# Weight pieces stored one place later in the queue, and weight sums computed in the second pass too

## The chip, the cores and the metric

The kernel runs on one core of one Trainium2 chip. The metric is device time in microseconds (us) of one execution, the median of the runs shown. A core has five engines that work side by side, each through its own instructions in order: TensorE (PE in the profile; PEld is its weight load), VectorE (DVE), ScalarE (ACT), GpSimd (POOL) and SyncE (SP), which here does little but issue transfers. Engines wait for each other, and for transfers, by semaphores. An instruction that waits holds up everything behind it on its engine.

## The reference

Three stages follow one another, all in float32:

```python
scores = scale * (q @ k.T) * Dmat          # retention: decay gamma_h ** (i - j), causal
x = (scores @ v) -> 2304 rows of 512
p = domain_probs / domain_probs.sum(-1)
x1 = sum over 4 experts e of p[:, e] * (relu(x @ w1[e]) @ w2[e])      # 512 -> 1024 -> 512
logits = x1 @ w_gate                        # second layer: 8 experts, 288 rows each,
out[rows of e] = relu(x1[rows] @ w1[e]) @ w2[e]    # assigned by descending logits
```

## The kernel before

To keep float32 accuracy on TensorE, every operand of a large product is split into a high half and the remainder, its low half; a product is then three products. A split is a ScalarE copy (the high half) and a subtraction on GpSimd or VectorE (the low half).

The work has three stages: the retention (up to some 107 us of the span), the first expert layer (to about 860 us), and the routed second layer. The change touches the first expert layer only. It runs in three passes, u = 0, 1 and 2, over 768 rows each. A pass has 16 *pairs*, k = 16u to 16u + 15; a pair is one block of 256 hidden columns of one expert. All 16 blocks of w1 are the same in each pass, so block q % 16 is fetched again in each.

The first product x @ w1 is done with seven block products instead of eight, over sums of blocks of x and sums of blocks of w1. The steps of a pair are called a to g (`step`, L697); each is one product of six matmuls, accumulating into PSUM tiles P, Q and R. Between them stand `keep` (L683, ScalarE copies P into `sum1` to `sum3`: keep 1 after a, keep 2 after c, keep 3 after e) and `add` (VectorE adds a kept sum to Q or R). P must be kept before the next product is accumulated into it, so step c waits for keep 1, step e for keep 2 and step f for keep 3. `y_next` (L837) puts a tile of the second product (12 matmuls, L727) between b and c, between d and e and between e and f.

**Weights of the first product.** `w1_load(q)` (L372) is issued at the end of pair q - 2. In the first pass it fetches the two raw blocks r1 from `w1a`. `w1_ops(q)` (L386) then makes six tiles: `wah`/`wal` from the first block, `wbh`/`wbl` from a sum held in place in the second block, `wth`/`wtl` from three sums in `tw` (128 x 768). Its first steps are `wah` and four VectorE subtractions (L397), which make the sums. `w1_store(q)` (L381) writes the sums to the scratch tensor `ts`. In the second and third passes `w1_load` fetches the first raw block, and the sums from `ts` (one 128 x 512 and one 128 x 768 transfer), and `w1_ops` returns six steps instead of ten: `steps[:1] + steps[5:]`. The calls `some(3)`, `some(3)`, `some(2)`, `some(2)` emit the steps after c, after d, after e and before f. The r1 tiles have two buffers for two blocks, so the next `w1_load` waits until the low halves of the block before are made; `tw` has one.

**Pieces of the second layer's weights.** While the first two passes run, all weights of the second layer are split ahead of time: 128 pieces of 128 x 512, 64 in each pass, by the generator `halves` (L436). For piece c it copies the high half on ScalarE (`pair`, L447), makes the low half on GpSimd (L448), then issues the store of piece c - 1 (L453 or L455) and the load of piece c + 2 into `pv` (L433). Both tiles have three buffers. `spare(main)` (L854) is called nine times in a pair, before and after most steps; five of these calls have main true, and each advances `halves` by one piece. The calls with main false do something only in the third pass.

Other transfers on SyncE's queue in a pair: two raw w2 blocks (`w2_load`, L659, k and 0 after step b, k and 1 ahead of step c), the loads and stores of `block_sums` (L866, called by `more_sums` after steps c and f), and the rows of x1 at the end of a pass. The order of all this is written out by hand in the loop over k (L898). At the *turn*, the last pair of a pass (`turn_`), the pieces must be done, and the x blocks of the next pass are loaded and split.

Of the kernel before, what the change touches and what calls it, by code (L numbers as in the profile page):

```python
# [144 lines left out]
class Graph:  # L145
# [87 lines left out]
    def copy(self, out, x, func=AF.Copy, part=False):  # L233
        self.add("act", 0.08 + self.size(x) / 1200.0, lambda: self.nc.scalar.activation(out, x, func), (x,), (out,),
                 part=part)
# [92 lines left out]
def tile_kernel(ctx, tc, a, x1d, xs, ss, ts, w1s, w2s, out):  # L328
    nc = tc.nc
# [16 lines left out]
    if True:  # L346
# [23 lines left out]
        WO, R1, TW = {}, {}, {}  # L370

        def w1_load(q, which=(0, 1)):  # L372
            e, j = divmod(q % 16, 4)
            for i in which:
                R1.setdefault(q, {})[i] = wl.tile([128, 512], F32, name="r1", bufs=2)
                nc.sync.dma_start(R1[q][i], a["w1a"][e, 2 * j + i] if q < 16 or i == 0 else ts[q % 16, :, :512])
            if q >= 16:
                TW[q] = wl.tile([128, 768], F32, name="tw")
                nc.sync.dma_start(TW[q], ts[q % 16, :, 512:])

# [5 lines left out]
        def w1_ops(q):  # L386
            ra, rb = (lambda: R1[q][0]), (lambda: R1[q][1])
            b11, b21, b12, b22 = (lambda: ra()[:, :256]), (lambda: ra()[:, 256:]), (lambda: rb()[:, :256]), (lambda: rb()[:, 256:])

            def w(i, h):  # L390
                if q not in WO:
                    WO[q] = [[wl.tile([128, n], F32R, name=f"w{x}{y}", bufs=2) for y in "hl"]
                             for x, n in (("a", 512), ("b", 512), ("t", 768))]
                return WO[q][i][h]

            t = lambda i: tt()[:, i * 256:(i + 1) * 256]
            sub = lambda e, o, x, y: lambda: e.tensor_tensor(o(), x(), y(), op=OP.subtract)  # L397
            copy = lambda i, x: lambda: nc.scalar.activation(w(i, 0), x(), AF.Copy)  # L398
            low = lambda e, i, x: lambda: e.tensor_tensor(w(i, 1), x(), r32(w(i, 0)), op=OP.subtract)  # L399
            v, p = nc.vector, nc.gpsimd  # L400

            def tt():
                if q not in TW:
                    TW[q] = wl.tile([128, 768], F32, name="tw")
                return TW[q]

            steps = [("act", 0.51, copy(0, ra), ("ra",), (f"wah{q}",)),
                    ("v", 0.33, sub(v, lambda: t(0), b12, b11), ("ra", "rb"), ("tw0",)),
                    ("v", 0.33, sub(v, b12, b22, b12), ("rb",), ("rb",)),
                    ("v", 0.33, sub(v, lambda: t(1), b22, lambda: t(0)), ("rb", "tw0"), ("tw1",)),  # L410
                    ("v", 0.33, sub(v, lambda: t(2), b21, lambda: t(1)), ("ra", "tw1"), ("tw2",)),
                    ("pool", 1.18, low(p, 0, ra), ("ra", f"wah{q}"), (f"wal{q}",)),
                    ("act", 0.72, copy(2, tt), ("tw0", "tw1", "tw2"), (f"wth{q}",)),
                    ("v", 0.86, low(v, 2, tt), (f"wth{q}", "tw0", "tw1", "tw2"), (f"wtl{q}",)),
                    ("act", 0.51, copy(1, rb), ("rb",), (f"wbh{q}",)),
                    ("pool", 1.18, low(p, 1, rb), ("rb", f"wbh{q}"), (f"wbl{q}",))]
            return steps if q < 16 else steps[:1] + steps[5:]

        hp = pool(st_l, "hp")
        st_p = ExitStack()  # L420
# [5 lines left out]
        def piece_of(c):  # L426
            e, i = divmod(c // 2, 8)
            return e, i, slice(c % 2 * HW, c % 2 * HW + HW)

        def halves_load(c):  # L430
            e, i, o = piece_of(c)
            r = room[0].tile([128, HW], F32, name="pv")
            nc.sync.dma_start(r, (a["w1b"] if i < 4 else a["w2b"])[e, i % 4][:, o])  # L433
            HV[c] = r

        def halves(c0, c1, loaded=False):  # L436

            if not loaded:
                for c in range(c0, min(c0 + HA, c1)):
                    halves_load(c)  # L440
                yield
                yield
            for c in range(c0, c1 + 1):
                if c < c1:
                    r = HV[c]
                    pair = HV[c] = room[0].tile([128, 2, HW], F32R, name="pair")
                    nc.scalar.activation(pair[:, 0], r, AF.Copy)  # L447
                    nc.gpsimd.tensor_tensor(pair[:, 1], r, r32(pair[:, 0]), op=OP.subtract)  # L448
                if c > c0:
                    e, i, o = piece_of(c - 1)  # L450
                    pair = HV.pop(c - 1)
                    if i < 4:
                        nc.sync.dma_start(w1s[e, i][:, :, o], r32(pair))  # L453
                    else:
                        nc.sync.dma_start(w2s[e, i - 4][:, o], r32(pair[:, 1]))  # L455
                if c + HA < c1:
                    halves_load(c + HA)
                yield


        with ExitStack() as st:
# [152 lines left out]
            for i in (0, 1, 4, 3, 5, 2, 6):  # L614
                for op in x_split(xr, i, LOW[i]):
                    g.add(*op)
            g.floor = 50.0
            g.add("sp", 0.8, lambda: w1_load(0), (), ("ra", "rb"))
            for op in w1_ops(0):
                g.add(*op)  # L620
            g.bias = 0.0
            late_sp = [g.add("sp", 1.0, lambda: w1_store(0), ("rb", "tw0", "tw1", "tw2"), ())]
            late_sp.append(g.add("sp", 0.8, lambda: w1_load(1), (), ("ra", "rb")))
            for op in w1_ops(1):
                g.add(*op)
            late_sp.append(g.add("sp", 1.0, lambda: w1_store(1), ("rb", "tw0", "tw1", "tw2"), ()))
            late_sp.append(g.add("sp", 0.8, lambda: w1_load(2), (), ("ra", "rb")))
            for n in range(HA):
                late_sp.append(g.add("sp", 0.4, lambda n=n: halves_load(n), (), ()))
# [8 lines left out]
        with ExitStack() as st:  # L638
# [17 lines left out]
            def w2_load(q, i):  # L656
                e, j = divmod(q % 16, 4)
                W2[q, i] = [hp.tile([128, 512], F32, name="r2", bufs=2)]
                nc.sync.dma_start(W2[q, i][0], a["w2a"][e, 2 * j + i])  # L659
# [190 lines left out]
            later = late()  # L850
            HC = 64
            jobs = [halves(0, HC, True), halves(HC, NH)]

            def spare(main):  # L854

                if not open_ or k < 2:
                    return
                if k > 16 * NP1 - 16:
                    next(later, None)
                elif main:  # L860
                    next(jobs[min(u, 1)], None)


            BLOCKS = {0: (0, 0), 1: (0, 1), 2: (1, 1)}
# [33 lines left out]
            for k in range(NPAIR):  # L898
                u, kk = divmod(k, 16)
                turn_ = kk == 15 and u < NP1 - 1  # L900
                lone = k in (0, NPAIR - 2)
                early = w1_ops(k + 1) if 1 <= k < NPAIR - 1 else []

                def more_sums():
# [7 lines left out]
                def block(i):  # L912
                    raw[i] = room[0].tile([128, 2, TG], F32, name=f"raw{i}")
                    if i in BLOCKS:
                        row, col = BLOCKS[i]
                        nc.sync.dma_start(raw[i], xs[u, :, 2 * col:2 * col + 2, row * TG:(row + 1) * TG])
                    else:
                        nc.sync.dma_start(raw[i], ss[u, i - 3])
# [7 lines left out]
                if k not in (1, NPAIR - 1):  # L926
                    step(k, "a")
                if turn_:
                    for _ in jobs[u]:
                        assert False  # L930
                    for _ in sums_of[u]:
                        assert False
                    st_p.close()
                    open_ = False
                    room[0] = pool(st_p, f"blocks{u}")
                    w2_load(k, 0)
                    for i in (0, 1, 4):
                        block(i)
                full = lone
                if k:  # L940
                    put(k - 1, 0, 1, "R")
                spare(True)
                step(k, "b")
                if not turn_:
                    w2_load(k, 0)
                spare(False)
                put(k, 0, 0, "Q")
                if not open_ and kk == 0:
# [4 lines left out]
                if turn_:  # L953
                    for i in (3, 5, 2, 6):
                        block(i)
                spare(True)
                step(k, "c")
                some(10 if full else 3)
# [76 lines left out]
    with ExitStack() as st:  # L1035
# [388 lines left out]
        for n, t in enumerate(range(NT - LATE, NT)):  # L1424
# [10 lines left out]
            else:  # L1435
                x = last[t - NT + K1]
# [80 lines left out]
```

## Time and profile before

| | us |
|---|---|
| Timed runs | 1154.66, 1157.22, 1160.98 (median 1157.22) |
| Profiled execution, its own time | 1154.98 |
| Span from the first to the last instruction | 1153.2 |
| TensorE busy | 1133.4 (98%) |
| TensorE weight load busy | 988.5 (86%) |
| VectorE busy | 705.6 (61%) |
| GpSimd busy | 632.0 (55%) |
| ScalarE busy | 561.2 (49%) |

The shares are averages over stages with different limits. The matmuls' ends are modelled, so a busy TensorE is not a TensorE at its peak: a weight load that comes late can lengthen a product without showing as idle time. The chain of work that ended last leads through TensorE's products in the third pass, and through transfers (w2 blocks, `pv` pieces, `tw`) in the first two.

### The profile page before, as it was taken

The page shows a single profiled execution, that of the slowest core. Times are in us where ns is not written, and L with a number is a line of the kernel's source. Part 1 is how long each engine was busy: PE and PEld are TensorE (multiplying, and loading weights), DVE is VectorE, ACT ScalarE, POOL GpSimd, SP SyncE. Part 2 cuts the span into 40 slices and gives each one's busy share as a digit, 9 for nine tenths or more (in the row PEclk, how much of TensorE's full clock was granted, in tenths as well). Part 3 has the DMA queues.
Part 4 walks back from the last instruction along what each step waited for, and adds up shares of the span by engine and source line. Part 5 has one row for each costly group of instructions (what it writes and reads, how often), then busy time and mean ns, then how long its engine had stood idle before and what let it go on. Part 6 is the DMA issues. An engine that isn't in the chain of part 4 may idle for free.

```text
span 1153.2 us, 22293 instructions
## 1 busy us (share of the span) xinstructions
PE 1133.4 (98%) x8007; PEld 988.5 (86%) x8007; DVE 705.6 (61%) x1632; ACT 561.2 (49%) x1262; POOL 632.0 (55%) x563
## 2 busy tenths in 40 slices
PE   9999999999999999999999999999999999999997
PEld 7878899989898998988899999998987888788886
DVE  4696777767665444544456777776347766666421
ACT  3444555555565555555554666666430333333341
POOL 4551576677774576666645999998231112222311
PEclk9999999999999999999999999999999999999999
DMA  9675699999994889898974655555214877788690
GB/s 330 219 248 176 234 338 344 322 319 321 345 309 144 279 286 335 290 310 302 316 262 158 221 181 195 192 180 158 78 55 167 311 292 284 307 332 334 252 409 27
DMA packets 131056, 292.99 MB, mean 254 GB/s; under 512 B 14849, under 2 KB 26881, under 8 KB 126849
## 3 DMA queue, kind: packets, MB, share of 16 engines
q1 hardware_dynamic: 127584, 281.88, 69.3%
q0 software_dynamic: 3216, 9.67, 2.4%
q8 instruction: 63, 1.03, 0.4%
q14 instruction: 49, 0.39, 0.1%
q10 hardware_dynamic: 144, 0.02, 0.0%
HBM read 214.41 MB, written 77.33 MB: 253 GB/s over the span
## 4 chain that ended last, share of the span: by engine, by line
PE 56%; DMA 15%; issue 5%; POOL 5%; DVE 3%; ACT 3%; SPq 3%; POOLq 0%; ACTq 0%; DVEq 0%
PE py L727 16%; PE ph L227 10%; PE P L677 9%; PE py L227 8%; PE R L677 5%; DMA r<-in_w2a 4%; DMA pv<-in_w1b 3%; DMA pv<-in_w2b 3%; DMA tw<-w_sums 3%; PE Q L677 2%; POOL pair L448 2%; PE pr L227 2%; DMA r<-in_w1a 1%; POOL w2l L665 1%; ACT pair L447 1%
## 5 line engine op out<-in xcount | busy, mean ns | idle before, releaser
L727 PE MATMUL py<-w2h,h 128*128 128x512 f32 x1056 | 349.5, 391 | 0.9 <-ACT h L694 0.8
L727 PEld LDWEIGHTS py<-w2h,h 128*128 128x128 f32 x1056 | 198.2, 188 | 40.4 <-ACT h L694 1.7
L448 POOL TENSOR_TENSOR pair<-pv,pair 128x512 fp32r<-128x512 f32 x128 | 177.3, 1391 | 97.4 <-ACT pair L447 93.4
L727 PE MATMUL py<-w2l,h 128*128 128x512 f32 x528 | 206.3, 391 | 0.0
L399 POOL TENSOR_TENSOR wal<-r,wah 128x512 fp32r<-128x512 f32 x48 | 66.8, 1392 | 87.1 <-ACT wah L398 71.8
L727 PEld LDWEIGHTS py<-w2l,h 128*128 128x128 f32 x528 | 99.2, 188 | 16.0
L684 ACT ACTIVATE sum<-P 128x384 f32<-128x384 f32 x144 | 70.0, 486 | 87.1 <-PE P L677 86.7
L665 POOL TENSOR_TENSOR w2l<-r,w2h 128x512 fp32r<-128x512 f32 x64 | 85.7, 1338 | 44.7 <-ACT w2h L664 44.7
L447 ACT ACTIVATE pair<-pv 128x512 fp32r<-128x512 f32 x128 | 80.2, 627 | 55.6 <-DMA pv<-in_w1b 27.2
L734 DVE SCALAR_TENSOR_TENSOR acc<-py,pr,acc 128x512 f32<-128x512 f32 x115 | 85.6, 745 | 29.8 <-PE py L727 29.5
L399 DVE TENSOR_TENSOR wtl<-tw,wth 128x768 fp32r<-128x768 f32 x48 | 63.5, 1322 | 64.4 <-ACT wth L398 64.2
L827 POOL TENSOR_TENSOR pp<-pw,wgb 128x512 f32<-128x512 f32 x64 | 98.5, 1560 | 1.4 <-DMA r<-in_w2a 1.4
L399 POOL TENSOR_TENSOR wbl<-r,wbh 128x512 fp32r<-128x512 f32 x48 | 81.1, 1690 | 14.6 <-ACT wbh L398 11.2
L695 DVE SCALAR_TENSOR_TENSOR h<-Q,h 128x384 fp32r<-128x384 f32 x96 | 53.4, 556 | 51.2 <-ACT h L694 51.2
L227 PE MATMUL ph<-gh,ub 128*128 128x288 f32 x512 | 83.3, 300 | 0.4 <-DVE gl L254 0.4
L664 ACT ACTIVATE w2h<-r 128x512 fp32r<-128x512 f32 x96 | 60.2, 628 | 42.2 <-DMA r<-in_w2a 42.1
L227 PEld LDWEIGHTS ph<-gh,ub 128*128 128x128 f32 x512 | 72.2, 188 | 1.2 <-DVE gl L254 0.7
L1299 POOL DMA_INDIRECT xg<-x_rows,idx x14 | 15.9, 1135 | 100.5 <-DVE idx L254 65.6
L534 ACT ACTIVATE Y<-s 64x128 f32<-64x128 f32 x128 | 33.8, 270 | 59.0 <-PE s L525 55.1
L694 ACT ACTIVATE h<-Q 128x384 fp32r<-128x384 f32 x96 | 46.7, 486 | 30.5 <-DVE Q L688 29.7
L507 POOL TENSOR_TENSOR Y<-Y,gk 64x576 f32<-64x576 f32 (+2 forms) x36 | 38.6, 1091 | 36.7 <-DMA Y<-in_kv 28.2
L523 PE MATMUL s<-X,Y 64*64 64x64 f32 x576 | 56.7, 228 | 2.0 <-DVE X L536 1.2
(272 smaller groups left out, 2667.7 us busy)
## 6 DMA issues: line engine op xcount, KB each, us to landing
w_halves<-pair SPq DMA_DIRECT2D x64, 512.0 KB, 6.0
ub<-w_halves SPq DMA_DIRECT2D x32, 1024.0 KB, 9.5
r<-in_w2a SPq DMA_DIRECT2D x96, 256.0 KB, 5.1
r<-in_w1a SPq DMA_DIRECT2D x64, 256.0 KB, 4.9
pv<-in_w1b SPq DMA_DIRECT2D x64, 256.0 KB, 5.6
pv<-in_w2b SPq DMA_DIRECT2D x64, 256.0 KB, 5.4
w_low<-pair SPq DMA_DIRECT2D x64, 256.0 KB, 4.8
raw<-in_w2b SPq DMA_DIRECT2D x32, 512.0 KB, 7.5
```

What stands on the lines that cost most here:

```text
L227: self.add("pe", cost, lambda: self.nc.tensor.matmul(out, w, x, start=start, stop=stop, **kw), (w, x), (out,), chain=chain, cols=self.size(x))
L399: low = lambda e, i, x: lambda: e.tensor_tensor(w(i, 1), x(), r32(w(i, 0)), op=OP.subtract)
L447: nc.scalar.activation(pair[:, 0], r, AF.Copy)
L448: nc.gpsimd.tensor_tensor(pair[:, 1], r, r32(pair[:, 0]), op=OP.subtract)
L523: nc.tensor.matmul(score()[:, h], Y[lo, h, ch(c + 1)], X[lo, h, ch(c + 1)], start=True, stop=True)
L664: nc.scalar.activation(h, r, AF.Copy)
L665: (nc.vector if i and q < 2 * NPAIR // NP1 else nc.gpsimd).tensor_tensor(lo, r, r32(h), op=OP.subtract)
L677: nc.tensor.matmul(PS[k][o][:, :TG], wx[:, c:c + 128], xx[:, kk], start=(start and n == 0), stop=(stop and n == 5), skip_group_check=True)
L684: nc.scalar.activation(sums[n], PS[k]["P"][:, :TG], AF.Copy)
L727: mm(y, x, w, start=(start and n == 0), stop=(stop and n == len(todo) - 1), **kw)
L734: nc.vector.scalar_tensor_tensor(x, y, s, x, op0=OP.mult, op1=OP.add)
L827: nc.gpsimd.tensor_tensor(pp, w[g, f], G0[e], op=OP.mult)
```

## The change

Two edits. (1) The limit from which stored weight sums are used moves from q = 16 to q = 32: in the second pass `w1_load` fetches both raw blocks, and `w1_ops` has all ten steps. The sums are still stored in the first pass, for the third. (2) `halves` yields True between the split of a piece and the store of the piece before; `spare` remembers this in `owed`, and its next call, main or not, issues the store of piece c - 1 and the load of piece c + 2, ahead of the next split.

```diff
-                nc.sync.dma_start(R1[q][i], a["w1a"][e, 2 * j + i] if q < 16 or i == 0 else ts[q % 16, :, :512])
-            if q >= 16:
+                nc.sync.dma_start(R1[q][i], a["w1a"][e, 2 * j + i] if q < 32 or i == 0 else ts[q % 16, :, :512])
+            if q >= 32:
                 TW[q] = wl.tile([128, 768], F32, name="tw")
                 nc.sync.dma_start(TW[q], ts[q % 16, :, 512:])
...
-            return steps if q < 16 else steps[:1] + steps[5:]
+            return steps if q < 32 else steps[:1] + steps[5:]
...
                     nc.gpsimd.tensor_tensor(pair[:, 1], r, r32(pair[:, 0]), op=OP.subtract)
+                yield True
                 if c > c0:
...
+            owed = []
             def spare(main):
                 if not open_ or k < 2:
                     return
                 if k > 16 * NP1 - 16:
                     next(later, None)
-                elif main:
-                    next(jobs[min(u, 1)], None)
+                elif main or owed:
+                    job = jobs[min(u, 1)]
+                    if owed:
+                        owed.pop()
+                        next(job, None)
+                    if main and next(job, None):
+                        owed.append(True)
...
                 if turn_:
-                    for _ in jobs[u]:
-                        assert False
+                    owed.clear()
+                    assert not [x for x in jobs[u] if x]
```

## Rows read from the trace of the kernel before

**Rows 1.** Busy time by stretches: passes one, two, three, the turn; last, DMA share, GB/s
```profile
core 0: us, PE busy (x) PEld busy (x) DVE busy (x) ACT busy (x) POOL busy (x), PEclk, DMA share, GB/s
128.00:345.00 217.00, 215.44 (x1080) 193.78 (x1079) 156.45 (x226) 122.82 (x234) 155.28 (x109) 1.00 0.94 329
376.00:604.00 228.00, 224.90 (x1137) 201.50 (x1136) 112.98 (x179) 126.05 (x241) 142.99 (x107) 1.00 0.87 297
620.00:785.00 165.00, 165.00 (x835) 149.85 (x834) 123.16 (x211) 101.98 (x245) 152.94 (x102) 1.00 0.60 202
335.00:351.00 16.00, 16.00 (x82) 14.37 (x81) 10.21 (x13) 10.79 (x19) 12.91 (x7) 1.00 0.76 280
```

**Rows 2.** Timeline of TensorE, step f: start us, us, instruction
```profile
138.65 0.51 PE L677 MATMUL P<-x2h,wth 128*128 128x384 f32 x2
...
342.68 0.51 PE L677 MATMUL P<-x2h,wth 128*128 128x384 f32 x2
...
444.61 0.51 PE L677 MATMUL P<-x2h,wth 128*128 128x384 f32 x2
...
604.75 0.51 PE L677 MATMUL P<-x2h,wth 128*128 128x384 f32 x2
...
790.72 0.51 PE L677 MATMUL P<-x2h,wth 128*128 128x384 f32 x2
```

**Rows 3.** Waits of TensorE and its weight load, second pass: total, times, longest
```profile
PEld P L677 <- ACT sum L684: 5.8, 7, 1.3
...
PE P L677 <- ACT sum L684: 2.9, 5, 0.9
```

**Rows 4.** Timeline of ScalarE ahead of a stall of step f, [idle before <- releaser]
```profile
504.59 0.85 ACT L398 ACTIVATE wth<-tw 128x768 fp32r<-128x768 f32 x1 [1.52 <-DMA tw<-w_sums]
...
507.17 0.63 ACT L664 ACTIVATE w2h<-r 128x512 fp32r<-128x512 f32 x1 [1.22 <-DMA r<-in_w2a]
...
508.23 0.47 ACT L684 ACTIVATE sum<-P 128x384 f32<-128x384 f32 x1
```

**Rows 5.** Waits of SyncE's queue, 376 to 604 us (second pass)
```profile
SPq L455 <- POOL pair L448: 33.1, 13, 4.8
SPq L453 <- POOL pair L448: 24.4, 12, 5.0
```

**Rows 6.** Waits of SyncE's queue, 128 to 345 us (first pass)
```profile
SPq L455 <- POOL pair L448: 26.3, 24, 2.8
SPq L453 <- POOL pair L448: 23.2, 23, 3.0
SPq L384 <- DVE tw L397: 9.5, 11, 2.0
SPq L383 <- DVE tw L397: 8.5, 8, 1.6
```

**Rows 7.** VectorE's subtractions of line 397, busy time in the first pass
```profile
128.00:345.00 217.00, 39.01 (x52) 1.00 0.94 329
```

**Rows 8.** One of the four subtractions, first pass: shortest, median, longest in ns
```profile
L397 DVE TENSOR_TENSOR r<-r x13: 424/1327/1344, 131.8 to 322.4; 128x256 f32<-128x256 f32 x13
```

**Rows 9.** Loads of pieces (`pv`), first pass: from issue to landing, us
```profile
DMA to landing us min/median/max: 3.1/5.4/7.4
```

**Rows 10.** Timeline of ScalarE: a pair's fifth piece and keep 1
```profile
314.61 0.62 ACT L447 ACTIVATE pair<-pv 128x512 fp32r<-128x512 f32 x1
...
315.50 0.49 ACT L684 ACTIVATE sum<-P 128x384 f32<-128x384 f32 x1
```

**Rows 11.** Timeline of SyncE: the last store of `w1_store`, tightest and last of 12 pairs
```profile
294.81 0.33 SPq L384 DMA_DIRECT2D w_sums<-tw  x1
...
310.39 0.33 SPq L384 DMA_DIRECT2D w_sums<-tw  x1
```

**Rows 12.** Timeline of TensorE: the step c that follows each of these
```profile
301.93 0.51 PE L677 MATMUL P<-x4h,wth 128*128 128x384 f32 x2
...
318.61 0.51 PE L677 MATMUL P<-x4h,wth 128*128 128x384 f32 x2
```

## The prediction

> **What bounds the kernel now.** I first read the busy time by stretches [rows 1]: in three stretches of the first expert layer the clock is at its full level and TensorE is busy for 215.4 of 217, 224.9 of 228 and 165.0 of 165 us. So TensorE sets the time, and the change can only give back what TensorE loses in the passes that it touches. "Busy" hides a part of that, since a late weight load lengthens a product without showing idle time. So I next measured the loss by the period of a pair: the times at which step f (the product P<-x2h) begins [rows 2]. In the third pass 12 pairs run from 604.75 to 790.72 us, that is 15.50 us each, and I take this as the undisturbed period. In the second pass the ten pairs from 444.61 to 604.75 take 160.14 us, 5.1 more than 10 x 15.50. In the first, the 13 pairs from 138.65 to 342.68 take 204.03, 2.5 more than 13 x 15.50. **The purse is therefore 5.1 + 2.5 = 7.6 us**, two thirds of a per cent of the run, whatever else the change does.
>
> Third, who takes it. In the second pass TensorE waits five times, each time at step f for ScalarE's copy `sum` (keep 3), 2.9 us of plain idle time; its weight loads wait for the same copy, 5.8 us in seven waits that overlap with these [rows 3]. This is the 5.1 us. The copy was late because ScalarE, which works in order, had stood still for data [rows 4]: 1.52 us for `tw` (the stored weight sums), 1.22 us for the raw w2 block. Fourth, why the data was late. SyncE issues nearly all transfers in order, and in the second pass it stood 33.1 + 24.4 = 57.5 us of 228 at the store of a weight piece, because GpSimd had not yet made its low half [rows 5]; every load behind it in the queue stood too. In the first pass it is 26.3 + 23.2 = 49.5 us, and another 9.5 + 8.5 = 18.0 us at `w1_store`, which waits for VectorE's weight sums [rows 6].
>
> **Second pass: sums computed, not loaded.** *Removed:* per pair one load of `tw`, 128 x 768 x 4 bytes = 0.39 MB; the other block is fetched from the weights in place of the stored sums, at the same size. At 297 GB/s [rows 1] a 15.5 us pair moves 4.60 MB; without 0.39 it is 4.21, or 272 GB/s, between the first pass (329) and the third (202). One issue fewer on SyncE goes with it. *Added:* four VectorE subtractions per pair. The first pass runs 13 such sets in 39.01 us [rows 7], so 3.0 us a pair. VectorE is busy 113.0 of 228 us in the second pass, 7.7 of 15.5 per pair [rows 1]; it becomes 10.7, 69%, against 156.5 of 217 = 72% in the first pass, which lives with it. So their time is covered by VectorE's idle time; uncovered, VectorE's add in step e would come late and step g would wait for it.
>
> Here a subtraction took 424 ns at least and 1327 ns in the middle of 13 [rows 8]. The Trainium skill, SBUF — State Buffer, section Who interferes with whom, says that a VectorE instruction with two SBUF inputs and a GpSimd instruction that reads SBUF shut each other out for the whole instruction; it speaks against this half of the change, and the spread in the row agrees with it. From the rows alone the four cost between 4 x 0.424 = 1.7 and 4 x 1.344 = 5.4 us per pair; even 5.4 fits into 7.8 us of idle time, but in one piece it could still delay the add (rival 2).
>
> *Moved:* with ten steps instead of six, the splitting of the second-pass weights spreads over the pair as in the first pass. Ahead of keep 3, ScalarE then has only the copy of `wa`; `wth` (0.85 us and its 1.52 us wait) and `wbh` go behind it [rows 4]. That is the very place where the five stalls arise. The price that is not in the trace is what the second pass still loses afterwards: at best nothing, as the third pass; at worst what the first pass loses with the same steps and more transfers, 2.5/13 = 0.19 us a pair or 1.9 in ten. The gain is 3.2 to 5.1; since 272 GB/s lies about midway between 202 and 329, I take the middle, **4.2 us**.
>
> **Both passes: store and load of a piece one place later.** Nothing is added or removed; each piece's store, *and the load of the piece two further on, which follows it*, are queued at the next `spare` place. By the order of the code they pass these: w2_load(k, 0), the transfers of the block sums, and in the first pass `w1_store`. They don't pass w1_load. (a) The raw w2 block is now requested ahead of one store's wait instead of behind it. That is what ScalarE waits for in the first pass, too, so it may recover up to the 2.5 us there; I take 2.0, since one or two GpSimd operations of lead remove most, but not all, of such a wait. In the second pass the gain is already in the 4.2. (b) The store waits for the same GpSimd operation as ever, and SyncE now reaches it later, so the stall mostly vanishes; what is late next is named in (c). (c) In the first pass the load of the pair's fifth piece now stands behind `w1_store`, which waits for VectorE. After that wait come the last sum store (0.33 us) and the piece's own store (taken as the same), then the landing, L, between 3.1 and 7.4 us with 5.4 in the middle [rows 9]. Only then can ScalarE do the piece, the copy of `h` and keep 1, 315.99 - 314.61 = 1.38 us [rows 10], which the next step c needs. So from the issue of the last sum store to the next step c, 0.7 + L + 1.38 = 2.1 + L must fit. Between them there were 7.1 us in the tightest of 12 pairs and 8.2 in the last [rows 11, 12]; the 12 are 9.8, 10.8, 10.5, 10.0, 10.2, 8.2, 8.9, 7.3, 7.8, 8.3, 7.1 and 8.2. With L = 5.4 the overruns sum to 0.6 us, with 6.0 to 2.1, with 7.4 to 10.7. I take 2.0: loads here land a little later than their middle, because the first pass has the DMA engines busy at 0.94 [rows 1]. **The first pass nets 2.0 - 2.0 = 0**, between -10.7 and +2.5.
>
> **The turn** into the second pass also computes sums now, in its most crowded pair. There VectorE is busy 10.2 of 16 us and GpSimd 12.9 [rows 1]. The 3.0 us fit into 5.8 idle ones; `wtl` shifts behind keep 3. No row shows the result: 0 if covered, 3.0 if not, and no gain, since no load there is awaited by TensorE. I take **-0.3**, near the covered end.
>
> **Sum.** 4.2 + 0 - 0.3 = 3.9 us. The profiled execution took 1154.98 us, 1153.2 of span and 1.8 around it, so it would take 1151.1. It lies 2.2 below the median of the three timed runs, 1157.22. The middle of all four (1154.66, 1154.98, 1157.22, 1160.98) is 1156.1; from there the forecast is **1152.2 us**.
>
> **Rivals.**
> 1. *Both passes run clean*: the loads come so early that all stalls go, 7.6 us: 1148.5. For it: all stalls that the trace shows in the second pass have one cause, which both edits hit. Against: the first pass has the transfers of before, at 0.94 busy, and earlier requests then only queue longer.
> 2. *The wait moves*: in the second pass the four subtractions, which stand in order on VectorE and wait for freshly loaded blocks, make the add of step e late instead of keep 3. If each of the ten pairs then loses what the five stalled ones cost now, nothing is gained: 1156, within 1.5 of before. For it: the first pass has such stalls. Against: it has them rarely, 2.5 us in 13 pairs. (The skill's rule on the shared exclusion, above, would bring this case about.)
> 3. *Slower*: (c) decides. Where loads queued behind `w1_store` land after 7.4 us, the first pass pays 10.7 and the sum is 4.2 - 10.7 - 0.3 = -6.8: 1162.9. With the 2.0 recovered by (a), the point from which it turns to a loss is an overrun of 5.9 us in sum, which the 12 gaps give at L = 6.7. For it: 7.4 was seen. Against: the middle is 5.4, and stores that lag also thin the queue.
> 4. *It doesn't do what it says*, if the store were still reached before GpSimd's work is done: then the second half gives nothing, and the first half its 4.2: 1152, the forecast again.
>
> **How the numbers follow.** Forecast (with rival 4) 0.48, clean 0.20, moved wait 0.20, slower 0.12. A measurement of this kernel can tell about 0.5% or 5.8 us from no change. Of the clean case nearly all, and of the forecast its upper quarter (the second pass wholly clean and some of the first), are faster by that: 0.33. Slower by that is rival 3: 0.12. The rest, 0.55, is within. The range reaches down to the clean case from the faster of the runs, 1154.98 - 7.6 = 1147.4, and up past the moved wait into the lower half of the slow case, 1159.
>
> **What would show it.** Right: the period of step f in the second pass at 15.5 to 15.7 us in every pair, no wait of step f for keep 3, SyncE's wait at the piece stores under 15 us in either pass, no `tw` load there, VectorE near 69%. Wrong in the first pass: ScalarE waiting for `pv` by 1 to 4 us ahead of `h` and keep 1, and TensorE waiting at step c. Wrong in the second: step g waiting for VectorE's add. The prediction falls if the first pass loses over 6 us, or the second still over 3.

## The result and the profile after

Over 17 runs each, the changed kernel took 1168.23 us (median) and the kernel before 1157.97. The ratio is 1.0083, with a 95% interval from 1.0062 to 1.0104. **The change makes the kernel slower by 0.8%**, some 10 us, where 0.3% faster was forecast. The profiled execution of the changed kernel has a span of 1164.4 us, 11.2 more than before.

The busy time by stretches shows that the two passes went opposite ways. These are the lines that answer to [rows 1]: first, second and third pass, each shifted by what was lost ahead of it. The columns are the same (span, PE, PEld, DVE, ACT, POOL, clock, DMA share, GB/s).

```profile
128.00:361.00 233.00, 220.11 (x1084) 195.43 (x1083) 171.03 (x231) 122.95 (x236) 155.50 (x109) 0.99 0.86 304
392.00:615.00 223.00, 223.00 (x1139) 202.53 (x1138) 169.32 (x231) 125.24 (x242) 148.94 (x107) 1.00 0.83 284
631.00:796.00 165.00, 165.00 (x834) 149.69 (x833) 125.52 (x210) 102.42 (x245) 151.12 (x102) 1.00 0.62 201
```

TensorE is busy for all of the second pass now (223.00 of 223), but idle for 12.9 us of the first. The granted clock is 0.99 and 1.00 of full in these rows, as before, so it is no part of this. The beginnings of step f, as in [rows 2], give the whole loss:

```profile
139.94 0.51 PE L678 MATMUL P<-x2h,wth 128*128 128x384 f32 x2
...
359.15 0.51 PE L678 MATMUL P<-x2h,wth 128*128 128x384 f32 x2
...
461.16 0.51 PE L678 MATMUL P<-x2h,wth 128*128 128x384 f32 x2
...
615.96 0.51 PE L678 MATMUL P<-x2h,wth 128*128 128x384 f32 x2
```

A pair that nothing disturbs takes 15.48 us, as every pair of the new second pass does. Against 13 x 15.48 the first pass loses 219.21 - 201.24 = 18.0 us (2.8 before); against 10 x 15.48 the second loses 154.80 - 154.80 = 0.0 (5.3 before). That is +15.2 and -5.3; another 1.3 us were lost ahead of pair 2, mostly in the retention stage, which the change does not touch. Together they are the 11.2 us. The table further down gives the loss of the two passes in this way, from one profiled execution of each kernel; the sums in it are 52 to 56 instructions. Code that is the same in three kernels (the first pass of before, of e2 and of e11) lost 2.8, 0.9 and 0.2 us, which is how far a profile can be trusted here.

What TensorE waits for in the first pass (128 to 345 us) is new too; columns: total, times, longest. Before, there were 0.9 us for keep 3 and 0.6 us for VectorE's add.

```profile
PE py L728 <- ACT h L695: 7.8, 4, 3.3
PE R L678 <- DVE Q L689: 4.4, 4, 1.6
PE P L678 <- ACT sum L685: 0.7, 1, 0.7
```

The longest of these waits shows how the loss arises. SyncE's queue, ScalarE and TensorE around it:

```profile
257.01 0.33 SPq L384 DMA_DIRECT2D w_sums<-tw  x1
257.43 0.54 SPq L454 DMA_DIRECT2D w_halves<-pair  x1
258.02 0.61 SPq L433 DMA_DIRECT2D pv<-in_w1b  x1
```

```profile
263.51 0.63 ACT L447 ACTIVATE pair<-pv 128x512 fp32r<-128x512 f32 x1 [3.71 <-DMA pv<-in_w1b]
264.05 0.47 ACT L695 ACTIVATE h<-P 128x384 fp32r<-128x384 f32 x1
264.42 0.48 ACT L685 ACTIVATE sum<-P 128x384 f32<-128x384 f32 x1
266.41 0.49 ACT L695 ACTIVATE h<-R 128x384 fp32r<-128x384 f32 x1 [1.51 <-DVE R L689]
...
266.95 0.50 PE L728 MATMUL py<-w2h,h 128*128 128x512 f32 x1 [3.33 <-ACT h L695]
...
267.88 0.52 PE L678 MATMUL P<-x4h,wth 128*128 128x384 f32 x2
```

Read from the top: `w1_store` ends with the store of `tw` at 257.01. Behind it stand the store and the load that follow the split of the pair's third piece: by the code the store of the second piece, and the load of the fifth, issued at 258.02, which lands 5.4 us later. (The expectations of e3 and e5 call the piece stored the fifth or the third; it is the second.) ScalarE has waited 3.71 us for it, with the ends of steps f and g queued behind. Its copy `h<-R` is ready at 266.90, and the last three matmuls of the y tile behind step b, which multiply with just this h, begin at 266.95. Step c follows at 267.88.

And why `w1_store` waited: VectorE makes the sums beside three subtractions of GpSimd.

```profile
251.72 1.43 DVE L397 TENSOR_TENSOR tw<-r,r 128x256 f32<-128x256 f32 x1 [1.16 <-DMA r<-in_w1a]
253.26 1.33 DVE L397 TENSOR_TENSOR r<-r 128x256 f32<-128x256 f32 x1
254.52 0.55 DVE L886 TENSOR_TENSOR cy<-cx,cy 128x384 f32<-128x384 f32 x1
254.99 2.00 DVE L397 TENSOR_TENSOR tw<-r,tw 128x256 f32<-128x256 f32 x2
```

```profile
251.59 1.29 POOL L399 TENSOR_TENSOR wal<-r,wah 128x512 fp32r<-128x512 f32 x1 [0.39 <-ACT wah L398]
252.97 1.34 POOL L666 TENSOR_TENSOR w2l<-r,w2h 128x512 fp32r<-128x512 f32 x1
254.95 1.29 POOL L448 TENSOR_TENSOR pair<-pv,pair 128x512 fp32r<-128x512 f32 x1 [0.64 <-ACT pair L447]
```

The first two sums took 1.43 and 1.33 us; the shortest such subtraction in [rows 8] took 0.424. The same line as [rows 7], between 128 and 345 us: 52 subtractions took 39.01 us before and take 59.35 now.

```profile
128.00:345.00 217.00, 59.35 (x52) 0.99 0.86 305
```

The last two of the four show it best. Shortest, median and longest in ns, before:

```profile
L397 DVE TENSOR_TENSOR tw<-r,tw x26: 410/424/1532, 132.1 to 324.1; 128x256 f32<-128x256 f32 x26
```

and in the changed kernel:

```profile
L397 DVE TENSOR_TENSOR tw<-r,tw x26: 417/1422/1535, 133.4 to 340.8; 128x256 f32<-128x256 f32 x26
```

Which subtractions of GpSimd moved beside the sums can be added up from the two engines' timelines. Of the sums' time some 16 us lay beside `wal`, before as now; beside `w2l` it was some 6 us and is 14, and beside the low halves of the pieces some 6 and is 23. So most of what was added comes from the pieces.

### The profile page after: what moved, and what is told of

Same layout as the page of the kernel before. It is cut to its first block, busy times and chain, and to the rows that moved or that the text cites. A ratio compares the mean times of both kernels' runs of the same rounds, so it can differ in the third digit from the quotient of the medians.

```text
span 1164.4 us, 22335 instructions
## 1 busy us (share of the span) xinstructions
PE 1135.3 (97%) x8007; PEld 990.0 (85%) x8007; DVE 780.7 (67%) x1696; ACT 559.9 (48%) x1262; POOL 636.3 (55%) x563
## 4 chain that ended last, share of the span: by engine, by line
PE 68%; DMA 4%; issue 4%; DVE 3%; POOL 2%; SPq 1%; ACT 1%; POOLq 0%; DVEq 0%; ACTq 0%
PE py L728 23%; PE P L678 12%; PE ph L227 10%; PE py L227 8%; PE R L678 6%; PE Q L678 3%; DMA r<-in_w1a 2%; PE pr L227 2%; DVE tw L397 2%; PE ph L231 1%; PE Q L763 1%; DMA pv<-in_w2b 1%; DMA pv<-in_w1b 1%; POOL pair L448 1%; DMA raw<-in_w2b 1%
## 5 line engine op out<-in xcount | busy, mean ns | idle before, releaser
L448 POOL TENSOR_TENSOR pair<-pv,pair 128x512 fp32r<-128x512 f32 x128 | 180.3, 1409 | 122.2 <-ACT pair L447 116.6
L666 POOL TENSOR_TENSOR w2l<-r,w2h 128x512 fp32r<-128x512 f32 x64 | 89.3, 1396 | 26.9 <-ACT w2h L665 26.8
L399 POOL TENSOR_TENSOR wbl<-r,wbh 128x512 fp32r<-128x512 f32 x48 | 76.7, 1598 | 15.4 <-PE py L728 6.5
L397 DVE TENSOR_TENSOR tw<-r,tw 128x256 f32<-128x256 f32 x64 | 69.1, 1080 | 1.2
L399 DVE TENSOR_TENSOR wtl<-tw,wth 128x768 fp32r<-128x768 f32 x48 | 56.3, 1172 | 15.7 <-ACT wth L398 15.5
```

What stands on the lines that cost most here:

```text
L666: (nc.vector if i and q < 2 * NPAIR // NP1 else nc.gpsimd).tensor_tensor(lo, r, r32(h), op=OP.subtract)
```

## The experiments

**The theory after the result**: two things act together in the first pass. The load of the fifth piece (and a store) stands behind `w1_store`, and `w1_store` comes later, since the sums are stretched by GpSimd. **Rivals**: the stores are harmful by being late, wherever they stand; the crossing alone is enough; both edits are needed for the loss.

| kernel | first pass loses | second pass loses | sums (line 397), 128 to 345 us | median, us | before beside it | ratio (95%) |
|---|---|---|---|---|---|---|
| before | 2.8 | 5.3 | 39.0 | 1157.97 | - | 1 |
| changed | 18.0 | 0.0 | 59.4 | 1168.23 | 1157.97 | 1.0083 (1.0062 to 1.0104) |
| e1, later places only | 19.5 | 5.0 | 60.6 | 1175.06 | 1156.43 | 1.0171 (1.0110 to 1.0232) |
| e2, computed sums only | 0.9 | 0.0 | 39.3 | 1151.90 | 1156.43 | 0.9951 (0.9922 to 0.9980) |
| e3, sum store behind | 0.0 | 0.0 | 53.8 | 1150.94 | 1156.43 | 0.9957 (0.9928 to 0.9985) |
| e4, load in place | 8.6 | 0.7 | 56.2 | 1155.98 | 1156.43 | 1.0000 (0.9973 to 1.0028) |
| e5, sum store ahead | 5.6 | 0.0 | 43.9 | 1155.32 | 1155.76 | 0.9999 (0.9972 to 1.0025) |
| e6, store in place | 8.4 | 1.4 | 56.7 | 1157.92 | 1155.76 | 1.0023 (0.9996 to 1.0050) |
| e7, ahead in odd pairs | 9.9 | 0.0 | 54.2 | 1161.00 | 1155.76 | 1.0038 (1.0006 to 1.0070) |
| e8, ahead in even pairs | 8.2 | 0.0 | 57.8 | 1156.26 | 1155.76 | 1.0002 (0.9977 to 1.0028) |
| e9, no reads beside the sums | 0.3 | 0.0 | 31.1 | 1149.83 | 1153.86 | 0.9965 (0.9941 to 0.9989) |
| e10, the same, as long | 0.0 | 0.0 | 26.4 | 1149.90 | 1158.96 | 0.9943 (0.9916 to 0.9970) |
| e11, steps spread only | 0.2 | 7.0 | 39.1 | 1158.10 | 1156.09 | 1.0018 (1.0000 to 1.0037) |

### Each half alone: e1 and e2

e1 is the changed kernel with the limits back at 16; e2 is the kernel before with the limits at 32 (its edit is shown, cut at the left; e1's runs the other way):

```diff
-  ... a["w1a"][e, 2 * j + i] if q < 16 or i == 0 else ts[q % 16, :, :512])
-            if q >= 16:
+  ... a["w1a"][e, 2 * j + i] if q < 32 or i == 0 else ts[q % 16, :, :512])
+            if q >= 32:
...
-            return steps if q < 16 else steps[:1] + steps[5:]
+            return steps if q < 32 else steps[:1] + steps[5:]
```

> Only the second edit: stores and loads of pieces one place later, weight sums loaded in the second pass as before. Theory (the loads of pieces now stand behind the sum stores of the first pass, which wait for VectorE): the whole loss of the first pass comes with this edit alone, so its 13 pairs lose 12 to 18 us as in the changed kernel (15.2 more than before's 2.8), and the time is 8 to 16 us above before. Rival (the loss needs both edits, say by the turn or by VectorE): the first pass loses under 5 us. The second pass tells whose the gain of 5.3 us is: under 1 us lost if it is the later place, about 5 if it is the sums.

> Only the first edit: the second pass computes its weight sums, pieces stored at the old place. Theory: the first pass is as before (2 to 4 us lost in 13 pairs, nothing in it is touched), the second pass loses 0 to 2 us instead of 5.3, so the time is 3 to 6 us below before. Rival (the second pass was mended by the later stores alone): it still loses 4 us or more and the time is that of before.

Both came as the theory had them, e1 (four runs; the others have ten) above its range, e2's first pass somewhat below its 2 to 4 us. The halves don't mix: **the later places cost the first pass (19.5 us) and give the second nothing (5.0); the computed sums give the second its whole 5.3 and leave the first alone.** e2 is faster than before by 0.5%.

### The crossing taken away: e3

```diff
                     split(1)
-                if 0 < k and k + 1 < 16:
-                    w1_store(k + 1)
                 spare(False)
+                if 0 < k and k + 1 < 16:
+                    w1_store(k + 1)
```

> The changed kernel with w1_store moved behind the spare place that follows it, so that the store and load of the pair's fifth piece no longer stand behind its wait for VectorE; all else as in the changed kernel. Theory: the first pass loses 0 to 4 us instead of 18, the second stays clean, and the time is 4 to 8 us below before, 13 to 18 below the changed kernel. Rival (the loss is from the store being later as such: the tiles of a pair come free later, or from the other transfers that it was moved past): the first pass still loses over 10 us.

Every one of the 13 pairs takes 15.48 us, within 0.02. The stores are still late, and the sums still stretched (53.8 us), but nothing that ScalarE needs stands behind them. So late stores as such do no harm, nor do stretched sums. SyncE still waits for the sums, with less behind it:

```profile
SPq L384 <- DVE tw L397: 25.9, 11, 3.8
SPq L456 <- POOL pair L448: 14.1, 16, 1.8
SPq L454 <- POOL pair L448: 12.1, 11, 2.2
```

### The load or the store: e4 and e6

e4, the load at its old place:

```diff
+                if c + HA < c1:
+                    halves_load(c + HA)
                 yield True
                 if c > c0:
...
-                if c + HA < c1:
-                    halves_load(c + HA)
                 yield
```

e6, the store at its old place:

```diff
-                yield True
                 if c > c0:
...
+                yield True
                 if c + HA < c1:
                     halves_load(c + HA)
```

> The changed kernel with the load of piece c + 2 issued at its old place, right after the split of piece c, and only the store of piece c - 1 one place later. Theory (the late load is what costs): the first pass loses 1 to 5 us, as before; SyncE again waits about 50 us of the first pass for GpSimd, now at the load, since the buffer that it fills is the one that GpSimd still reads. Rival (the late store is what costs, by the pair tiles that wait for it): the first pass loses over 10 us as in the changed kernel.

> The changed kernel with the store of piece c - 1 back at its old place and only the load of piece c + 2 one place later, the other half of e4. Theory (load and store each cost when they stand behind w1_store; the late store alone cost 8.4 us in the first pass): the late load alone costs 8 to 15 us there, ScalarE waiting for pv. Rival (it takes the late store to make the loads late): the first pass loses under 4 us.

Neither theory nor rival has the number of e4: 8.6 lies between their ranges. e6 is at the lower edge of the theory's. Either half costs about half. In e4 ScalarE waits for what it did not wait for before, the landing of the stores, whose tiles the next pieces need:

```profile
ACT pair L447 <- DMA w_halves<-pair: 20.6, 18, 2.5
```

In both the sums are stretched (56 to 57 us). Since the lost times are so alike, and each also has the loads in another order, I take from these two only that the load is not the sole carrier.

### The crossing by itself: e5

```diff
                 w2_split(k, 0)
+                if 0 < k and k + 1 < 16:
+                    w1_store(k + 1)
                 spare(True)
...
-                if 0 < k and k + 1 < 16:
-                    w1_store(k + 1)
                 spare(False)
```

> The kernel of e2 (sums computed in the second pass, pieces stored and loaded at their old places) with one thing moved: w1_store is issued ahead of the spare place that it used to follow, so that only the store of the pair's third piece and the load of its fifth stand behind its wait. This adds the suspected cost by itself. Theory (that crossing is the whole loss): the first pass loses 8 to 18 us where e2 loses 0.7, the second stays clean, and the time is 4 to 14 us above before. Rival (the other places passed, or the later places together, are needed for the loss): the first pass loses under 4 us and the time is that of e2.

It loses 5.6, between the two, and 4.7 more than e2, from which it differs by this alone: the crossing by itself gives under a third of the loss, and the theory that it is all of it falls. Here the sums take 43.9 us, hardly more than before's 39.0. Over the pairs 3 to 13, the store of `tw` is issued 13.8 us after the preceding step f in e5, 13.9 before, and 16.1 in the changed kernel. The missing part goes with those 2.2 us: in the changed kernel the sums begin 0.4 us later than before and run 1.8 us longer.

### Which pairs: e7 and e8

Both start from e3. This is e7; e8 has `k % 2 == 0`:

```diff
+                if 0 < k and k + 1 < 16 and k % 2:
+                    w1_store(k + 1)
                 spare(False)
-                if 0 < k and k + 1 < 16:
+                if 0 < k and k + 1 < 16 and not (k % 2):
                     w1_store(k + 1)
```

> The kernel of e3, with w1_store ahead of the spare place again in the odd pairs of the first pass only. Theory (the late piece holds up ScalarE's work for the end of the pair, and the y tile behind step b of the next pair needs that work only when the next pair is even, for it starts on two pairs just ended): nearly the whole loss of the changed kernel returns, 8 to 17 us in the first pass, in the even pairs 4 to 14. Rival (every late piece costs; pairs without loss are those that profit from the stall just paid): about half, 5 to 9 us, as in e8.

> The kernel of e3, with w1_store ahead of the spare place in the even pairs of the first pass only. Theory (the pair that follows is odd, and its first y tiles use older pairs, so only keep 1 before step c can be late): the first pass loses 0 to 4 us. Rival (every late piece costs): 5 to 9 us, as in e7.

By size the rival is nearer: e8 loses 8.2 where the theory gave it at most 4. But the kinds of wait are two, and divided as the theory has it. In e7 TensorE waits mainly at a y tile, in pairs 4, 8, 10 and 14; in e8 never there, but at step g. First e7, then e8:

```profile
PE py L728 <- ACT h L695: 4.9, 4, 2.4
PE R L678 <- DVE Q L689: 0.8, 1, 0.8
```

```profile
PE R L678 <- DVE Q L689: 5.2, 6, 1.5
PE P L678 <- ACT sum L685: 0.6, 1, 0.6
```

So the late piece reaches the y tile only where the next pair is even (in the changed kernel, too, these waits are in pairs 6, 8, 10 and 14). In e8 the second carrier shows, at step g of odd and even pairs (5, 6, 7, 10, 11 and 13): VectorE's add, which step g needs, stands behind the four sums. One of these, where the four run from 216.66 to 221.93:

```profile
216.66 0.97 DVE L397 TENSOR_TENSOR tw<-r,r 128x256 f32<-128x256 f32 x1 [0.64 <-DMA r<-in_w1a]
217.73 1.33 DVE L397 TENSOR_TENSOR r<-r 128x256 f32<-128x256 f32 x1
218.99 2.94 DVE L397 TENSOR_TENSOR tw<-r,tw 128x256 f32<-128x256 f32 x2
221.85 0.74 DVE L735 SCALAR_TENSOR_TENSOR acc<-py,pr,acc 128x512 f32<-128x512 f32 x1
222.51 0.55 DVE L689 TENSOR_TENSOR Q<-R,sum 128x384 f32<-128x384 f32 x1
```

### The stretched sums taken away: e9 and e10

In the first pass (q from 3 to 15 for `wal`, k from 2 to 14 for `w2l`), e9 lets GpSimd write zeros where it would subtract. e10 writes them two and a half times, to be busy as long (columns 512, 512 and 256).

```diff
-("pool", 1.18, low(p, 0, ra), ...
+("pool", 1.18, low(p, 0, ra) if not 2 < q < 16 else lambda: p.memset(r32(w(0, 1)), 0.0), ...
...
+                if i == 0 and 1 < q < 15:
+                    nc.gpsimd.memset(r32(lo), 0.0)
+                    return
```

> The changed kernel; in the first pass two GpSimd subtractions per pair, the low halves wal and (for the first w2 block) w2l, are replaced by GpSimd writing zeros there, so that part of the low halves is left out of the result. Same queues and waits; GpSimd then reads no SBUF beside VectorE's weight sums except for a piece. Theory (the later places also cost through the sums: since the w2 block arrives earlier, GpSimd's subtractions fall beside the four sums and stretch them from 39 to 59 us in the stretch from 128 to 345 us, which delays w1_store): the sums take 25 to 42 us and the first pass loses 2 to 9 us instead of 18. Rival (the crossing at w1_store is enough by itself, the stretched sums are only its consequence): it still loses 12 us or more.

> As e9 (part of the low halves of the first pass left out), but GpSimd writes the zeros two and a half times, so that it is busy about as long as with the subtraction, 1.3 us, and still reads no SBUF. It tells whether e9 was clean because GpSimd no longer reads beside the sums or because GpSimd was free earlier. Theory (reading is what stretches the sums): line 397 takes 25 to 42 us between 128 and 345 us and the first pass loses 0 to 5 us. Rival (GpSimd's time): the sums are again above 50 us or the first pass loses 9 us or more.

They lose 0.3 us (e9, below its theory's 2 to 9) and 0.0 (e10, the lower end of its 0 to 5), **with the crossing in place as in the changed kernel**. In e10 GpSimd works as long as ever (149.8 us busy in the stretch), and the last two sums take their 0.42 us every time, where the changed kernel's median was 1422 ns:

```profile
L401 DVE TENSOR_TENSOR tw<-r,tw x28: 418/422/426, 132.3 to 333.7; 128x256 f32<-128x256 f32 x28
```

So GpSimd's reads stretch the sums, not its time. The Trainium skill, SBUF — State Buffer, section Who interferes with whom, says just this: a VectorE instruction with two SBUF inputs contends with a GpSimd instruction that reads SBUF, not with one that only writes it. This row and that of the changed kernel agree.

For the loss the two kernels show less than they seem to, for they go beyond undoing the stretch. The sums take less than before the change (31.1 and 26.4 us; 39.0 before), begin earlier, and the store of `tw` is issued 11.3 and 10.6 us after step f, where before had 13.9. By the code, writing zeros also waits neither for ScalarE's high half nor for the raw block, so the waits are not the same, though e9's expectation calls them so. What they show is that the crossing is free when `w1_store` is early. With the sums near those of before, the crossing costs what e5 lost.

### What mended the second pass: e11

```diff
+            none = [(None, 0, lambda: None, (), ())]
-            return steps if q < 16 else steps[:1] + steps[5:]
+            return steps if q < 16 else steps[:1] + (none * 4 if q < 32 else []) + steps[5:]
```

> The kernel of before, loads and stores untouched, the sums still loaded in the second pass; only the emission of the second pass's weight steps is spread as in the changed kernel (four empty steps stand where the sums would be computed), so that wth and wbh go behind keep 3 on ScalarE. Theory A (the second pass was mended because the wait for tw no longer stands ahead of keep 3): the second pass loses 0 to 1.5 us instead of 5.3, without one byte less. Theory B (it was mended by the 0.39 MB less per pair): it still loses 3.5 us or more. The first pass is as before, 1 to 4 us lost.

Theory A, on which the prediction stood, falls as a sufficient cause: with `wth` and `wbh` behind keep 3 and all bytes as before, the second pass loses 7.0 us. ScalarE now stands still for the w2 blocks instead (376 to 604 us before: 11.9 us in 12 waits; here between 392 and 604):

```profile
ACT w2h L665 <- DMA r<-in_w2a: 45.0, 13, 4.7
```

What separates e11 from e2 in the second pass is the transfer of `tw` that e2 does not make, 0.39 MB and one issue per pair, and the sums computed in its stead. So, with the steps spread, it is the removal of the transfer that mends. Whether by its bytes, its issue or the wait for it was not separated, and whether the removal would do without the spread steps was not run.

## Why the prediction was wrong, point by point

**The purse** (5.1 + 2.5; 5.3 + 2.8 by the period of 15.48) was right in size. The second pass gave back all that it had, and e3 and e10 have hardly a lost tenth of a microsecond in either pass.

**Second pass.** 4.2 us were forecast, 5.3 came. The sign, the place and the size were right; the reason was not. I named the place in ScalarE's order as what mends it, and e11 shows that this alone does nothing; it takes the removal of the transfer. That the number came so near is in part luck. The traffic was also reckoned wrongly: a pair of that pass took 16.0 us, not 15.5, so at 297 GB/s it moved 4.76 MB and not 4.60; less 0.39, over 15.48 us, that is 282 GB/s, and the row says 284, not 272. The four sums were covered by VectorE's idle time, as said: 169.3 of 223 us busy, 76% rather than 69%, and no wait at step g there.

**SyncE's waits were no measure of a cost.** The forecast was that they fall under 15 us at the piece stores. In the first pass they fell from 49.5 to 19.7, in the pass that got slower. In the second they rose from 57.5 to 73.3, in the pass that became clean. The second pass's lines that answer to [rows 5], 392 to 604 us:

```profile
SPq L456 <- POOL pair L448: 45.0, 26, 4.0
SPq L454 <- POOL pair L448: 28.3, 14, 4.0
```

SyncE waits longer there, and TensorE waits for nothing: between 392 and 615 us its idle time is nil. In the first pass SyncE now waits at `w1_store` instead, 32.2 + 25.4 = 57.6 us (18.0 in [rows 6]):

```profile
SPq L384 <- DVE tw L397: 32.2, 13, 4.0
SPq L383 <- DVE r L397: 25.4, 11, 3.0
SPq L456 <- POOL pair L448: 12.6, 12, 2.0
SPq L454 <- POOL pair L448: 7.1, 14, 1.6
```

**First pass, (a).** Right: the w2 block came earlier, and ScalarE's waits for it fell from 28.2 to 2.7 us (128 to 345 us). The lines, before and after:

```profile
ACT w2h L664 <- DMA r<-in_w2a: 28.2, 13, 3.4
```

```profile
ACT w2h L665 <- DMA r<-in_w2a: 2.7, 5, 0.9
```

But the same edit moved GpSimd's low halves, of the pieces above all and of w2, beside the sums, which was not thought of.

**First pass, (c), is the step that failed.** It named the right place, the fifth piece's load behind `w1_store`, and put 2.0 us on it, 10.7 at most, where the first pass lost 18.0. L was right: 5.4 us in the stall shown. Two terms were wrong, and one path was left out.

First, the issue time of the last sum store was taken from the trace of before [rows 11], as if the change left it alone. It comes 2.2 us later after step f (16.1 instead of 13.9), mostly because the sums take 59.4 us instead of 39.0. The sums' price was weighed for the second pass only, against VectorE's idle time in total; that the other edit changes what runs beside them in the first was not asked. e9 and e10 show that nothing is lost when that store is early (11.3 and 10.6).

Second, the consumer was wrong. I let keep 1 and step c be the first to need ScalarE, 1.38 us behind the piece. In even pairs the y tile behind step b needs `h<-R`, which is ready 266.90 - 263.51 = 3.4 us after the piece begins, and step c starts only 0.9 us after these last matmuls (267.88). That is 3.4 + 0.9 in the place of 1.38, 2.9 us more in every second pair.

Left out was step g: VectorE's add, late behind the stretched sums, held it for 4.4 us in four waits. At step c itself, where (c) looked for the whole cost, TensorE waited once, 0.7 us.

e5 is (c) as it was reckoned, with the store of `tw` at the time of before (13.8): it cost 4.7 us more than e2, so 2.0 was too small even there, though by little more than the 2.6 us by which equal first passes differ. The larger part of the 18.0 came with the later store.

**The turn** was put at -0.3. The three pairs from the turn's step f on take 55.57 us (359.15 to 414.72) against 55.49 before: nothing.

**The rivals.** Rival 3 came true in direction and place, with 0.12; its own price of 10.7 fell 7.3 short. Rival 2's mechanism, sums in order ahead of the add, came true too, but in the first pass, and it is not a rival to the third: they feed each other. Rival 1 describes e3 and e10. The upper end, 1159, would have had to take in the slow case's own 1162.9; even that fell short of 1168.23.

**What stays open.** How the 18 us divide between the load, the store and the add was not separated further: e4 to e8 lose 5.6 to 9.9 each, and the shares depend on one another, because a stall delays the next blocks and these the next sums. In the changed kernel the store of `tw` in pair 4 comes 14.0 us after the preceding step f, and 1.0 us is lost up to the next step f; in pair 5 it then comes after 17.8, and 3.1 are lost. For e9 and e10, how much is due to shorter sums and how much to their earlier start was not separated either.

## What to carry to other kernels

When an issue is moved behind another one in a queue, take the time at which that other one's wait ends from what the change makes of it, not from the trace of before, and follow the late data to the first consumer in the order of *every* engine behind it. A waiting queue is no cost by itself; ask who needs what stands behind it. And of two edits made at once, each should be priced in each stage: here one gave 0.5% and the other cost 1.7%, and the place of a single store (e3) makes the pair as fast as the good half alone.

## What the runs showed that I had not expected

A VectorE subtraction of 128x256 with both inputs in SBUF took 0.42 us beside a writing GpSimd and up to 1.5 us beside a reading one. So where GpSimd's subtractions fall decides whether four of them take 1.7 or over 5 us, and moving a transfer can move that. And with the sums computed and 8% less to move (0.39 of 4.76 MB a pair), the second pass had no stall left.
